# A new issue order for all five engines of a fused Infini-attention and spectral-filter kernel

## The chip, the cores and the metric

The kernel runs on one core of a Trainium2 chip. The core has a matrix engine (TensorE, in the profile PE, with its weight loads as PEld), three engines for elementwise work (VectorE or DVE, ScalarE or ACT, GpSimd or POOL), and SyncE (SP), which here only issues DMAs. Each engine takes its own queue of instructions strictly in order and waits on semaphores for the others. The metric is the device time of one launch in microseconds.

## The reference

Two branches share one input x of 2048 tokens by 640 channels, and a gate per token mixes them. Branch A is attention with a compressive memory: 32 heads of width 20, four segments of 512 tokens, exact softmax attention inside a segment and a running memory (M, z) over the segments before. Branch B is a two-dimensional spectral filter: a real FFT over tokens and channels, a product with complex weights, and the inverse.

```python
phi = lambda t: jnp.where(t > 0, t + 1.0, jnp.exp(t))
for s in range(N):                      # 4 segments
    logits = jnp.einsum('bhqd,bhkd->bhqk', qs, ks) * scale + mask
    p = _softmax(logits, axis=-1)
    a_dot = jnp.einsum('bhqk,bhkd->bhqd', p, vs)
    num = jnp.einsum('bhld,bhde->bhle', phi(qs), M)
    den = jnp.einsum('bhld,bhd->bhl', phi(qs), z)[..., None] + 1e-06
    outs.append(g * num / den + (1.0 - g) * a_dot)      # g = sigmoid(beta)
    M = M + jnp.einsum('bhld,bhle->bhde', phi(ks), vs)
    z = z + jnp.einsum('bhld->bhd', phi(ks))
a = o @ wo
...
b = irfft2(rfft2(x) * (w_r + 1j * w_i))
g = sigmoid((x * gate_w).sum(-1, keepdims=True))
out = g * a + (1 - g) * b
```

Inputs are bfloat16; the sums run in 32 bits.

## The kernel before

All work is first recorded as a list of operations, without an order: a matmul group into one PSUM bank, one copy out of a bank, one elementwise instruction, one DMA. Each operation knows what it reads and writes, and which engines may do it (one or two). Then `Sched.schedule` (from line 117) turns a list of numbers written out by hand, `Kern.ORDER` (from line 639), into a queue for each engine, and `Sched.emit` writes the instructions with their waits. The value v of the list stands for operation v // 2, and v % 2 says which of its engines does it:

```python
        for v in order:
            o = ops[v // 2]
            o.eng = list(o.alts)[v % 2]
            queue[o.eng].append(o)
```

Three more things follow from the order. First, the PSUM bank of each group: banks 0 to 3 are one slot of four banks for attention scores, banks 4 to 7 are single banks for everything else, and a group may only begin when its bank has been read out. Second, DMAs: a DMA is issued once no more than `WINDOW = 1600000` bytes of earlier ones are outstanding, and 56 semaphores are handed round among them. Third, the form of TensorE's tiles: whole 128 by 128, the 20 by 64 tiles of the scores, or columns of 128 by 32; a few groups may take either of two forms and follow their neighbours (line 565 is a matmul split into columns, line 567 an ordinary one).

*Branch A.* `project`, `proj_tile` and `v_tile` make q, k and v of each segment from the transposed x (xT, brought in by transposing DMAs, line 600). q and k go through DRAM: stores to `qk_scr` (`st_qk`), then DMAs `pad2` (line 602) that write the padded operand `qkp`, each of 40 KB in the first segment, eight of them for one set. phi(k) is transposed by a DMA into `pkn` (`pkT`, line 600). `qk_unit` does one of 73 score units into the four-bank slot, ACT turns it into exponentials (`ex`, line 1357), POOL masks the diagonal (line 1391), and `pv_flipped` and `pv_group` multiply by v. With the flipped form the denominators are gathered through DRAM (`dnc`) and inverted in one instruction (line 1294, `den_rec`); products then normalise the output (line 1645). `mem_read` (lines 1224 to 1229) and `mem_update` (operation `mupd`) work on the memory, and an addition joins both parts of the output (lines 1438 and 1655).

*Branch B.* `fft` is a chain of matmuls with constant tables (`fcat`, `big`, `tt`): the folded input (lines 972 and 977), stages F1 and D, the product with the weights (lines 1548 and 1553, `W_mul` and `W_add`), stage T and back; `fft_out` makes even and odd halves and adds them into G (line 1602, `sum_Db`).

*The end.* `finish_tile` multiplies the attention output by wo, the gated G by its last table, into one bank; `final` copies that out to `ot` (line 577 on ACT, line 579 on DVE), and DMAs store it. The gate table of each segment (`gate_tab`, line 1094) is broadcast by a DMA `ld_g`.

Copies out of PSUM may be done by ACT or DVE (`copy_alts`), many additions by DVE or POOL (`either`).

Of the kernel before, what the change touches and what calls it, by code (L numbers as in the profile page):

```python
# [510 lines left out]
class Kern:  # L511
# [84 lines left out]
    def dma(self, dst, src, nbytes, r, w, prio, tr=False, name="", after=(), queue="sp"):  # L596
# [43 lines left out]
        23, 0, 78, 28, 92, 74, 2, 4, 24, 6, 8, 26, 10, 12, 76, 14, 30, 16, 18, 20, 46, 34, 180, 44, 184, 52, 220, 208, 36, 196, 210, 186, 48, 198,  # L640
        212, 42, 188, 190, 222, 38, 94, 200, 202, 96, 204, 192, 224, 206, 99, 226, 195, 228, 214, 101, 216, 231, 542, 32, 262, 219, 103, 544, 302,
        264, 304, 80, 306, 368, 106, 308, 82, 266, 104, 370, 84, 268, 1618, 66, 270, 132, 372, 272, 386, 87, 310, 570, 274, 313, 388, 280, 572, 68,
        282, 276, 134, 50, 390, 284, 88, 286, 54, 108, 392, 394, 58, 90, 374, 110, 288, 396, 828, 830, 136, 558, 290, 833, 113, 376, 560, 822, 824,
        379, 834, 139, 827, 1620, 416, 836, 418, 70, 420, 140, 422, 838, 72, 424, 114, 496, 426, 498, 117, 294, 500, 502, 1622, 504, 550, 506, 246,
        296, 552, 342, 278, 248, 56, 232, 142, 234, 120, 292, 250, 252, 118, 344, 316, 122, 354, 318, 254, 298, 314, 346, 320, 356, 256, 124, 348,
        300, 144, 236, 350, 126, 238, 322, 352, 240, 1842, 128, 358, 168, 242, 360, 1844, 130, 362, 146, 244, 1624, 364, 1626, 1812, 149, 258, 1846,
        380, 1848, 1850, 1628, 546, 400, 40, 1852, 816, 818, 1630, 821, 1632, 260, 1814, 1634, 1816, 156, 366, 846, 848, 1818, 170, 850, 1642, 398,
        840, 150, 842, 1644, 332, 158, 844, 1820, 1646, 336, 152, 1648, 1822, 402, 1650, 154, 810, 404, 1662, 1652, 894, 382, 812, 1664, 172, 340,
        814, 1666, 384, 896, 328, 882, 160, 884, 898, 1668, 1658, 334, 888, 887, 890, 175, 1670, 338, 892, 566, 1673, 330, 442, 562, 1636, 444, 326,
        446, 1880, 1638, 448, 324, 568, 176, 1882, 508, 162, 510, 450, 512, 164, 514, 452, 454, 1656, 167, 516, 456, 458, 1654, 460, 518, 462, 179,  # L650
        470, 520, 412, 1884, 464, 1886, 522, 1888, 466, 472, 410, 474, 584, 1890, 476, 468, 478, 912, 578, 914, 480, 900, 902, 916, 608, 580, 905,
        414, 1868, 1870, 564, 610, 1872, 408, 1874, 1876, 1684, 1660, 934, 870, 1878, 1686, 182, 872, 1640, 1688, 406, 876, 875, 878, 574, 1690,
        1892, 880, 1692, 600, 586, 1695, 1896, 1676, 576, 1898, 602, 482, 1894, 484, 1900, 554, 1902, 938, 1904, 428, 906, 1906, 582, 430, 932, 908,
        486, 488, 548, 911, 490, 432, 434, 492, 436, 1680, 1854, 918, 2310, 494, 438, 920, 1678, 1856, 1858, 525, 440, 1860, 556, 1862, 922, 924,
        926, 588, 858, 860, 658, 928, 60, 863, 594, 1864, 1698, 526, 852, 1866, 804, 596, 1674, 854, 864, 806, 660, 936, 1934, 857, 1922, 1936, 1924,
        930, 1926, 1928, 1938, 1930, 62, 1940, 590, 1932, 2306, 694, 1942, 1724, 593, 1944, 604, 1726, 1946, 628, 1696, 1682, 866, 1022, 1948, 780,
        606, 630, 1728, 869, 1908, 782, 612, 1910, 1730, 1700, 1912, 1914, 1916, 784, 696, 1732, 788, 1918, 940, 942, 1734, 662, 1920, 1951, 614,
        944, 948, 950, 664, 1742, 1736, 952, 792, 947, 1953, 794, 955, 1738, 786, 1702, 1704, 796, 698, 960, 2308, 800, 956, 790, 962, 1706, 1740,
        529, 616, 798, 978, 1954, 1708, 958, 666, 598, 618, 1710, 980, 1957, 986, 531, 982, 988, 1713, 802, 1794, 990, 1796, 1959, 993, 1798, 1714,
        1800, 1718, 1756, 1716, 1016, 532, 985, 624, 620, 1758, 964, 626, 1802, 1720, 1760, 966, 534, 998, 1744, 1020, 1804, 1762, 536, 636, 1764,  # L660
        1000, 994, 1754, 1766, 1072, 638, 1074, 1076, 670, 996, 1824, 808, 1078, 974, 1024, 640, 672, 1774, 1988, 1002, 1776, 540, 1990, 642, 1778,
        977, 1780, 1722, 1004, 1782, 1770, 648, 1992, 632, 1994, 1784, 678, 1960, 651, 1768, 1970, 622, 1750, 1026, 2350, 680, 1972, 1786, 1028,
        1790, 1030, 2352, 1974, 644, 1033, 2354, 538, 968, 1976, 700, 1012, 1110, 970, 1772, 1006, 1015, 1748, 1008, 634, 1788, 686, 973, 646, 1104,
# [1064 lines left out]
```

## Time and profile before

| | us |
|---|---|
| median of 3 runs | 236.89 |
| lowest and highest | 235.61, 237.70 |
| the profiled execution | 235.84 |
| its span in the profile | 233.7 |

The profile shows one execution. Times are microseconds from the start of its span. For each engine it gives busy time; an entry of a timeline reads: start, length, engine, line, operation, result and inputs, count, and in brackets the idle time just before with the operation that ended it. SPq and ACTq are DMAs as their engine issues them; the length is that of the issue, and the landing comes later. A matmul's end is modelled, and successive matmuls overlap by some 0.1 us, so entries of TensorE overlap as well. A group of instructions reads: line, engine, operation, result and inputs with their shapes, count, then busy us in all and mean ns of one, then idle time before it and who ended it.

### The profile page before, as it was taken

The page shows a single profiled execution, that of the slowest core. Times are in us where ns is not written, and L with a number is a line of the kernel's source. Part 1 is how long each engine was busy: PE and PEld are TensorE (multiplying, and loading weights), DVE is VectorE, ACT ScalarE, POOL GpSimd, SP SyncE. Part 2 cuts the span into 40 slices and gives each one's busy share as a digit, 9 for nine tenths or more (in the row PEclk, how much of TensorE's full clock was granted, in tenths as well). Part 3 has the DMA queues.
Part 4 walks back from the last instruction along what each step waited for, and adds up shares of the span by engine and source line. Part 5 has one row for each costly group of instructions (what it writes and reads, how often), then busy time and mean ns, then how long its engine had stood idle before and what let it go on. Part 6 is the DMA issues. An engine that isn't in the chain of part 4 may idle for free.

```text
span 233.7 us, 10364 instructions
## 1 busy us (share of the span) xinstructions
PE 222.5 (95%) x4381; PEld 142.2 (61%) x4395; DVE 191.4 (82%) x486; ACT 194.0 (83%) x215; POOL 148.6 (64%) x301
## 2 busy tenths in 40 slices
PE   7899999999999999999999999899999989999994
PEld 2575676776546666554657554555645457767794
DVE  0299998789999997999999889999799975955364
ACT  2179898889999899999999989999989879788720
POOL 8153138366668985477766878488998758487700
PEclk9999999999999999999999999999999999999999
DMA  6999945999998978456984764685799743222524
GB/s 153 289 330 281 222 150 159 207 195 242 214 201 193 231 186 248 111 148 200 234 176 123 215 196 118 207 181 190 215 155 212 202 126 93 76 78 59 181 95 123
DMA packets 59265, 42.18 MB, mean 180 GB/s; under 512 B 30228, under 2 KB 55380, under 8 KB 59220
## 3 DMA queue, kind: packets, MB, share of 16 engines
q1 hardware_dynamic: 58180, 40.96, 69.7%
q8 instruction: 34, 0.56, 1.0%
q10 hardware_dynamic: 1040, 0.57, 0.9%
q14 instruction: 11, 0.09, 0.1%
HBM read 23.32 MB, written 12.30 MB: 152 GB/s over the span
## 4 chain that ended last, share of the span: by engine, by line
PE 68%; DVE 15%; ACT 5%; SPq 4%; DMA 4%; issue 2%; POOL 1%; DVEq 0%
PE psum L567 61%; PE psum L565 7%; ACT ex L1357 4%; DVE Pt L1548 3%; SPq L602 2%; DMA xsb<-in_A_x_dram 2%; DVE Cp L579 2%; SPq L600 2%; DMA dnc<-u_scr 2%; DVE G L1602 2%; DVE Bt L579 1%; DVE mem L1229 1%; DVE ub L579 1%; DVE Yt L1553 1%; ACT ub L577 1%
## 5 line engine op out<-in xcount | busy, mean ns | idle before, releaser
L1357 ACT ACTIVATE ex<-psum 128x2048 bf16<-128x2048 f32 (+1 forms) x73 | 135.2, 1853 | 11.7 <-PE psum L567 10.6
L1391 POOL TENSOR_SCALAR_AFFINE_SELECT ex<-ex 128x256 bf16<-128x256 bf16 (+3 forms) x224 | 104.5, 485 | 43.2 <-ACT ex L1357 12.1
L567 PE MATMUL psum<-qkp 20*64 20x64 bf16 (+5 forms) x1280 | 31.9, 270 | 1.8 <-DVE qkp L579 0.7
L567 PE MATMUL psum<-xT,wk 128*128 128x256 bf16 (+1 forms) x280 | 33.2, 273 | 0.3 <-DVE mem L1229 0.2
L567 PE MATMUL psum<-xT,wq 128*128 128x512 bf16 (+1 forms) x121 | 27.7, 380 | 1.6 <-DMA xT<-in_A_x_dram 0.8
L567 PE MATMUL psum<-wv,xT 128*32 128x321 bf16 (+3 forms) x385 | 27.8, 301 | 0.0
L1548 DVE TENSOR_TENSOR Pt<-psum,Wt 128x642 bf16<-128x642 f32 x32 | 25.4, 815 | 0.4 <-PE psum L567 0.3
L567 PEld LDWEIGHTS psum<-qkp 20*64 20x64 bf16 x1280 | 13.7, 103 | 17.4 <-ACT ex L1357 11.2
L567 PEld LDWEIGHTS psum<-xT,wk 128*128 128x128 bf16 (+1 forms) x280 | 20.0, 97 | 6.4 <-issue 1.6
L977 POOL TENSOR_TENSOR xsb<-xf 128x320 bf16<-128x320 bf16 (+2 forms) x11 | 8.4, 771 | 20.4 <-DVE xf L972 11.4
L567 PE MATMUL psum<-big,Cp 128*128 128x321 bf16 (+1 forms) x96 | 18.9, 303 | 1.1 <-DVE G L1602 0.9
L565 PE MATMUL psum<-wo,oU 128*32 128x320 bf16 x460 | 19.6, 299 | 0.0
L1187 DVE TENSOR_TENSOR va<-psum,ebx 128x320 bf16<-128x320 f32 x32 | 15.0, 483 | 4.3 <-PE psum L567 1.9
L567 PE MATMUL psum<-big,Ac 128*128 128x161 bf16 (+2 forms) x96 | 17.1, 257 | 0.7 <-DVE Pt L1548 0.3
L567 PE MATMUL psum<-ex,va 128*32 128x64 bf16 (+3 forms) x576 | 17.4, 256 | 0.1
L567 PEld LDWEIGHTS psum<-wv,xT 128*32 128x32 bf16 (+1 forms) x385 | 13.5, 96 | 6.3 <-issue 1.5
L567 PE MATMUL psum<-tt,Yt 128*128 128x256 bf16 (+1 forms) x96 | 16.3, 275 | 0.4 <-POOL Yt L1553 0.3
L567 PEld LDWEIGHTS psum<-ex,va 128*32 128x32 bf16 x576 | 10.9, 96 | 8.8 <-issue 0.7
L972 DVE TENSOR_TENSOR xf<-xsb 128x640 bf16<-128x640 bf16 x16 | 8.2, 515 | 9.1 <-DMA xsb<-in_A_x_dram 9.0
L1144 ACT ACTIVATE et<-qu 128x512 bf16<-128x512 bf16 x25 | 15.4, 625 | 0.2 <-DVE phq L1157 0.2
L1602 DVE TENSOR_TENSOR G<-eo,psum 128x320 bf16<-128x320 f32 x32 | 14.9, 480 | 0.7 <-PE psum L567 0.2
L579 DVE CAST Bt<-psum 128x322 bf16<-128x322 f32 x26 | 13.2, 517 | 2.1 <-PE psum L567 1.8
(102 smaller groups left out, 394.1 us busy)
## 6 DMA issues: line engine op xcount, KB each, us to landing
qkp<-qk_scr SPq DMA_DIRECT2D x28, 160.0 KB
tt<-tab_tt SPq DMA_DIRECT2D x8, 512.0 KB, 4.7
qk_scr<-qu SPq DMA_DIRECT2D x12, 256.0 KB, 3.8
u_scr<-ub SPq DMA_DIRECT2D x12, 256.0 KB, 4.3
xsb<-in_A_x_dram SPq DMA_DIRECT2D x8, 320.0 KB, 5.6
oU<-u_scr SPq DMA_DIRECT2D x15, 128.0 KB, 3.3
out_dram<-ot SPq DMA_DIRECT2D x12, 160.0 KB
Wt<-in_B_w_r_dram SPq DMA_DIRECT2D x16, 80.2 KB, 4.0
```

What stands on the lines that cost most here:

```text
L565: h = e.matmul(dst, wt, r_, start=st, stop=sp_, **{**kw, "tile_position": (0, q), "skip_group_check": True})
L567: h = e.matmul(o_, l_, r_, start=st, stop=sp_, **kw)
L579: alts["dve"] = (lambda e: e.tensor_copy(dst(), src()), 67 + 1.04 * n, 68.0)
L600: return e.dma_start_transpose(d_, s_)
L972: self.either(lambda e, r=r, op=op: e.tensor_tensor(xf.ap(r * 642, [321, 2], [1, 320]), xs.ap(o, [D, 2], [1, 320]), xs.ap(o + 320, [D, 2], ...
L977: self.either(lambda e, dst=dst, src=src, d0=d0, n=n, op=op: e.tensor_tensor(xs.ap(o + dst, [D, 2], [1, n]), xf.ap(src + d0, [321, 2], [1, ...
L1144: self.one("act", lambda e: e.activation(et.ap(0, [1, L]), qsl(), ACT.Exp), L, [qb], [b("et", pi_)], late, fix=95, name="phi_exp")
L1187: self.one("dve", lambda e: e.tensor_tensor(va.ap(i * H * VW + h0 * VW, [VW, nh], [1, DH]), self.ps(bank, 0, [DH, nh], [1, DH]), self.ebx. ...
L1357: self.one("act", lambda e, d=d, q=q: e.activation(self.ex.ap(*d), self.ps(bank, *q), ACT.Exp, scale=SC), 2048 if kind < 2 else 512 * n, [ ...
L1391: self.one("pool", lambda e: e.affine_select(self.ex.ap(*d, p0=p0, np_=np_), self.ex.ap(*q, p0=p0, np_=np_), [[0, 4], [1, n]], ALU.is_ge, ...
L1548: self.one("dve", lambda e, ri=ri, Pt=Pt, Wt=Wt, wo_=wo_, bank=bank: e.tensor_tensor(Pt.ap(ri * 322, [644, 2], [1, KD]), self.ps(bank, 0, ...
L1602: self.one("dve", lambda e, q=q, n2=n2, bank=bank, eo=eo: e.tensor_tensor(self.G.ap(n2 * D + 639 * q, [1 - 2 * q, 320]), eo.ap(q, [1, 320] ...
```

## The change

Only the list `Kern.ORDER` is replaced. The operations, their instructions, the tables, the buffers and all constants of the scheduler are the same. The new list names the same 2311 operations in another sequence, fourteen of them with their other engine. A few lines of the diff, which has 97 on one side and 96 on the other (332 is the `pad2` that the prediction speaks of, 324 the `pkT` near it):

```diff
     ORDER = (
-        23, 0, 78, 28, 92, 74, 2, 4, 24, 6, 8, 26, 10, 12, 76, 14, 30, 16, 18, 20, 46, 34, 180, 44, 184, 52, 220, 208, 36, 196, 210, 186, 48, 198,
...
-        840, 150, 842, 1644, 332, 158, 844, 1820, 1646, 336, 152, 1648, 1822, 402, 1650, 154, 810, 404, 1662, 1652, 894, 382, 812, 1664, 172, 340,
...
-        446, 1880, 1638, 448, 324, 568, 176, 1882, 508, 162, 510, 450, 512, 164, 514, 452, 454, 1656, 167, 516, 456, 458, 1654, 460, 518, 462, 179,
...
-        4524, 4512, 4510, 4554, 4556, 4527, 4566, 4508, 4558, 4568, 4560, 4546, 4570, 4548, 4572, 4563, 4574, 4542, 4544, 4577, 4506, 4580, 4582,
-        4584, 4578,
+        23, 0, 78, 28, 92, 74, 2, 4, 24, 6, 8, 26, 10, 12, 76, 14, 30, 16, 18, 20, 46, 34, 180, 44, 184, 48, 196, 186, 52, 188, 198, 190, 36, 220,
...
+        322, 1630, 244, 1814, 168, 400, 1850, 1632, 821, 260, 149, 1816, 1634, 398, 846, 130, 1852, 258, 848, 1818, 170, 850, 840, 842, 324, 1642,
...
+        510, 330, 512, 514, 164, 454, 1654, 1658, 448, 450, 176, 456, 458, 332, 452, 167, 1880, 516, 414, 460, 462, 518, 1882, 384, 470, 408, 520,
...
+        4532, 4613, 4502, 4598, 4486, 4534, 4505, 4488, 4520, 4616, 4618, 4522, 4491, 4550, 4552, 4614, 4536, 4538, 4512, 4554, 4556, 4506, 4541,
+        4564, 4620, 4524, 4566, 4510, 4558, 4527, 4568, 4508, 4560, 4570, 4572, 4542, 4563, 4544, 4574, 4577, 4546, 4548, 4578, 4584, 4582, 4580,
```

By engine, the lengths of the queues before and after are: PE 1066 and 1066, DVE 486 and 488, ACT 223 and 221, POOL 297 and 297, SP 239 and 239. The operations that go to another engine:

| operation | line | from | to |
|---|---|---|---|
| three `final` | 577, 579 | ACT | DVE |
| two `final` | 579, 577 | DVE | ACT |
| one `ev_D` (copy of a spectral stage, `Bt`) | 577, 579 | ACT | DVE |
| another `ev_D` | 579, 577 | DVE | ACT |
| one `ev_oT3` (copy of a transposed output, `oTl`) | 577, 579 | ACT | DVE |
| two `W_add` | 1553 | DVE | POOL |
| one addition to the attention output, at the end | 1438 | DVE | POOL |
| another such addition | 1438 | POOL | DVE |
| one fold of the input | 977, 972 | POOL | DVE |
| one small operation of the gate | 1060 to 1080 | POOL | DVE |

Operations that keep their place in their queue: 365 of 1066 on PE, 141 of 218 on ACT, 91 of 480 on DVE, 48 of 294 on POOL and 37 of 239 on SP. The mean move is 1.7 places on PE, 1.9 on DVE, 3.0 on POOL and 4.6 on SP. The form of TensorE's tiles changes 202 times in the new order, 206 times in the old one.

183 rows, old and new, of the table ORDER are left out of this document.

## The prediction

> **What bounds the kernel now.** I read the page's totals, its slices and the chain that ended last; then the busy time by windows and TensorE's waits; then the queue of SyncE and TensorE's timeline wherever a moved operation lies. From the page:
>
> ```profile
> span 233.7 us, 10364 instructions
> PE 222.5 (95%) x4381; PEld 142.2 (61%) x4395; DVE 191.4 (82%) x486; ACT 194.0 (83%) x215; POOL 148.6 (64%) x301
> PEclk9999999999999999999999999999999999999999
> q8 instruction: 34, 0.56, 1.0%
> PE 68%; DVE 15%; ACT 5%; SPq 4%; DMA 4%; issue 2%; POOL 1%; DVEq 0%
> ```
>
> The reader is to see an almost full TensorE at its full clock: 233.7 − 222.5 = 11.2 us is all that it idles, and an order can win little else, since the matmuls stay the same. Where that idle time is, TensorE's waits and two windows (columns: window, length, then busy us of PE, PEld, DVE, ACT, POOL; clock, DMA share, GB/s) tell:
>
> ```profile
> PE psum L567 <- DVE G L861: 1.3, 1, 1.3
> PE psum L567 <- DVE G L1602: 0.9, 1, 0.9
> PE psum L567 <- DMA xT<-in_A_x_dram: 0.8, 1, 0.8
> PE psum L567 <- DVE qkp L579: 0.7, 1, 0.7
> PE psum L567 <- ACT ex L1357: 0.6, 2, 0.4
> ...
> 105.00:125.00 20.00, 18.77 (x321) 11.02 (x321) 19.42 (x55) 19.04 (x18) 14.36 (x32) 1.00 0.78 188
> ...
> 220.00:233.70 13.70, 10.46 (x300) 9.21 (x288) 6.82 (x19) 2.73 (x6) 1.64 (x4) 0.98 0.36 108
> ```
>
> 1.3 and 0.8 us are the first wait and the first transposed tile of x, which the change leaves where they are; 13.70 − 10.46 = 3.2 us lie around the last matmuls and stores. So about 11.2 − 1.3 − 0.8 − 3.2 = 5.9 us are there to be won inside. The window 105 to 125 shows why a search finds it hard: DVE 19.42 and ACT 19.04 of 20 us, beside PE at 18.77.
>
> **The change, part by part.** Read out by engine, the new list has the same 1066 TensorE operations and the same 239 on SP. The exponentials' 73 score units keep their sequence; 365 TensorE operations keep their place and the others move by 1.7 places in the mean. SP is dealt anew: 37 of 239 keep their place, the largest moves are 24 places later and 38 earlier. I took SP first, since there an operation that is moved drags others with it.
>
> *The padded q and k of the first segment.* One of the eight DMAs that write the padded operand qkp goes from place 30 of SP to place 39, behind the transposing transfer of pkn that was at place 38, the seven others and a store:
>
> ```profile
> 29.25 4.86 SPq L602 DMA_DIRECT2D qkp<-qk_scr  x8
> 34.15 1.21 SPq L600 DMA_TRANSPOSE pkn<-phk  x1
> 35.46 0.54 SPq L602 DMA_DIRECT2D qk_scr<-qu  x1
> 36.11 2.48 SPq L602 DMA_DIRECT2D qkp<-qk_scr  x4
> ...
> L602 SPq DMA_DIRECT2D qkp<-qk_scr x12: 281/360/1835, 29.2 to 38.2; - x12
> ...
> 36.64 0.42 PE L567 MATMUL psum<-qkp 20*64 20x320 bf16 x16
> ...
> out_dram<-ot SPq DMA_DIRECT2D x8, 40.0 KB, 1.6
> qk_scr<-qu SPq DMA_DIRECT2D x12, 256.0 KB, 3.8
> ```
>
> In the new order there lie ahead of the piece the seven others (4.86 less a median issue of 0.36: 4.5, the one long issue of 1835 ns kept among them), the transfer (1.21), the store (0.54) and 0.1 of gaps: it is issued at 29.25 + 6.35 = 35.6. Landing: 1.6 us for the same 40 KB elsewhere, 3.8 for a larger transfer as the long end. So 35.6 + 1.6 = 37.2 to 35.6 + 3.8 = 39.4, against TensorE's need at 36.64, with the same matmuls ahead. The stall is 0.6 to 2.8 us; I take 0.9, near the end with the 40 KB row, since it has the size and SP issues little else at that time. TensorE takes its queue in order, so all of it counts unless a later wait hides it.
>
> The Trainium skill ("DMA: Bandwidth & Descriptors", Anatomy of one DMA) puts a fixed cost of about 2.0 us on every DMA, most of it the receipt of the write; by it the estimate is 35.6 + 2.0 = 37.6 and a stall of 1.0, where the row says 1.6 and 0.6.
>
> *Other late data.* The memory update below reads pkn, whose transfer moves one place down, behind an issue:
>
> ```profile
> 39.40 1.32 SPq L600 DMA_TRANSPOSE pkn<-phk  x1
> ...
> pkn<-phk SPq DMA_TRANSPOSE x9, 4.7
> ...
> 44.71 0.29 PE L567 MATMUL psum<-fcat,xsb 128*128 128x128 bf16 x2
> 44.83 0.43 PE L567 MATMUL psum<-va,pkn 128*128 128x154 bf16 x4
> ```
>
> By the median of such transfers it lands at 39.40 + 4.7 = 44.1, 0.7 ahead of 44.83. By the queue ahead of it it is issued 1.0 later: 0.3 late, but TensorE is by then 0.9 late itself, so 0 (0.3 if the first stall isn't there). A table for the T stage at 131 us and another memory update at 73 us come 0.3 to 0.4 late by the same walk down the queue. For all of these together I take +0.2, ends 0 and 1.1.
>
> *Tile forms.* The rows that follow hold TensorE (first four) and DVE (last two) around the denominators of a late segment:
>
> ```profile
> 186.29 0.45 PE L567 MATMUL psum<-big,Cp 128*128 128x321 bf16 x2
> 186.67 0.32 PE L565 MATMUL psum<-wo,oU 128*32 128x320 bf16 x4
> ...
> 190.18 0.72 PE L567 MATMUL psum<-big,Cp 128*128 128x321 bf16 x4 [0.94 <-DVE G L1602]
> 190.83 0.43 PE L567 MATMUL psum<-qkp 20*64 20x512 bf16 x12
> ...
> 188.30 0.95 DVE L1294 RECIPROCAL dnr<-dnc 128x128 f32<-128x128 bf16 x1 [1.58 <-DMA dnc<-u_scr]
> 189.17 0.95 DVE L1602 TENSOR_TENSOR G<-eo,psum 128x320 bf16<-128x320 f32 x2
> ```
>
> Four matmuls and a change of form take 190.83 − 190.18 = 0.65, two and a change 186.67 − 186.29 = 0.38; so a pair of matmuls is 0.27, and 0.11 remains for a change of form. The new order has 202 of them instead of 206: −0.44, none of it hidden on a full engine.
>
> *The reciprocal at 188.30.* DVE waits 1.58 us for the gathered denominators, computes 0.95, and only then frees the bank for which TensorE waits 0.94. In the new order a normalising product and the first of the two sums of G go ahead of the reciprocal; DVE does them in the wait and the bank is free sooner. The ends are 0 and −0.94; I take −0.4, because the second sum still follows the reciprocal and is late next.
>
> *The wait at 148.69 and the tail.*
>
> ```profile
> 148.69 0.42 PE L567 MATMUL psum<-qkp 20*64 20x320 bf16 x16 [0.43 <-ACT ex L1357]
> ...
> L1357 ACT ACTIVATE ex<-psum 128x2048 bf16<-128x2048 f32 x71 | 133.2, 1876 | 11.6 <-PE psum L567 10.6
> ```
>
> Some matmuls of the spectral stage move ahead of the score unit at 148.69 and fill its 0.43; they push the unit back, and the exponential behind it, so I count −0.3 (ends −0.43 and 0). In the tail an addition to the attention output goes from DVE to POOL and two transposes come earlier, but the last matmuls follow one another densely: −0.2, ends −0.7 and +0.5, the latter POOL's longer 790 against 317 ns from the rows below. The gate table for the last tiles is loaded six SP places later and still made ahead of its first matmul by my walk down the queues, so nothing (up to +1 if its load, too, lands late).
>
> *The engine changes.* Their prices by shape, one form on its two engines each:
>
> ```profile
> L1553 POOL TENSOR_TENSOR Yt<-Pt 128x321 bf16<-128x321 bf16 x16 | 11.6, 727 | 1.0 <-DVE phq L1156 0.4 <-DVE dn L1224 0.3 <-DVE Pt L1548 0.2
> L1553 DVE TENSOR_TENSOR Yt<-Pt 128x321 bf16<-128x321 bf16 x16 | 5.2, 328 | 0.4 <-PE psum L567 0.3
> L579 DVE CAST ot<-psum 128x320 bf16<-128x320 f32 x16 | 7.4, 489 | 6.5 <-PE psum L565 4.5 <-PE psum L567 1.5 <-DMA out_dram<-ot 0.4
> L577 ACT ACTIVATE ot<-psum 128x320 bf16<-128x320 f32 x16 | 6.5, 435 | 1.7 <-PE psum L567 0.9 <-PE psum L565 0.8
> L1438 DVE TENSOR_TENSOR on<-on,mem 128x320 bf16<-128x320 bf16 x7 | 1.9, 317 | 0.0
> L1438 POOL TENSOR_TENSOR on<-on,mem 128x320 bf16<-128x320 bf16 x1 | 0.8, 790 | 0.0
> ```
>
> Five of the fourteen are copies of output tiles (three to DVE, two to ACT: 54 ns each), two W additions and two attention additions go to POOL (+0.40 and +0.47 us each, if someone waits; DVE gets 0.3 back each), two are a pair of spectral copies that swap engines, and three small ones remain. POOL is busy 64%, and ACT and DVE 82 and 83%: as work this is a fair deal, as latency it is a small loss. Taken as 0, ends −0.6 (four times 0.3 off a full DVE, half of it felt) and +0.8 (both W additions late at the T stage).
>
> **The sum.** +0.9 + 0.2 − 0.44 − 0.4 − 0.3 − 0.2 + 0 = −0.24 us. The profiled execution took 235.84 us, its span 233.7, so 2.1 lie outside; the sum gives a span of 233.5 and 235.6 for this run. The median of the three runs before, 236.89, is 1.05 above the profiled one, and by the median the sum gives 236.65. I predict 236.6: no change. One per cent, 2.4 us, is about what a measurement here tells from none.
>
> **The rivals.** *Slower: the instruction blocks hit the wrong issues.* The long pad issue of 1835 ns coincides with a packet of the instruction queue q8; so does a transposing transfer that took a microsecond more than the one behind it:
>
> ```profile
> 66.40 2.28 SPq L600 DMA_TRANSPOSE pkn<-phk  x1
> ...
> 69.82 1.25 SPq L600 DMA_TRANSPOSE pkn<-phk  x1
> ```
>
> An SP issue is stretched by 1.0 to 1.5 us where a block is fetched. There are 34 such packets; in the order before the slack ahead of qkp and pkn takes them up, in the new one they fall on other issues. Each that falls ahead of an operand with less slack costs 0.9 to 1.3 of a full TensorE, as in the first part. One is in the sum; from the third the gains of 1.3 us are eaten, and with four the time is 236.65 + 3 × 1.1 = 239.9. For it: the two rows above, and 202 issues with new places. Against it: where I walked down the new queue, only one operand came late by more than 0.5.
>
> The Trainium skill ("Runtime: NRT & Kernel Launch", Instruction fetch mechanics) holds the opposite: the fetch of the next block is mostly hidden behind the rate at which instructions are issued; by that rule this rival has no price and the time stays at the forecast. The 1835-ns issue speaks against it, though that it coincides with a packet is no proof of the cause.
>
> *Faster: the idle time inside goes.* If a block falls elsewhere and no issue at 31 is stretched, the late piece of qkp leaves 1.5 us earlier, at 34.1, lands at 35.7 and stalls nothing. The first two terms (+1.1) fall away, and half of the 5.9 us of idle time inside, 2.9 instead of the 0.9 in my sum, can go: 236.65 − 1.1 − 2.0 = 233.5. For it: the new order puts free work into both of the waits that I looked at. Against it: DVE and ACT at 95 to 97% between 105 and 125, where a place that one operation gains is another's loss.
>
> *The change does nothing.* All stays in the same waits; 236.9, which is inside the forecast.
>
> **How the numbers follow.** Forecast, no change, 0.44 (own range 235.1 to 238.6: below, the qkp stall at 0.6 instead of 0.9, no other late data, the wait for G wholly gone and the tail at its good end, −0.3 − 0.2 − 0.5 − 0.5; above, the stall at 2.8, +1.9); faster 0.30, centred on 233.5, of which about 0.25 lies below 234.5; slower 0.26, centred on 239.9, of which 0.22 lies above 239.3. The forecast's own flanks give 0.02 and 0.03. Faster by over 1%: 0.27; within: 0.48; slower: 0.25. With about a tenth left out on either side the range is 233.4 to 239.9.
>
> **What would show it.** The score unit that now starts at 36.64 would show a wait of 0.6 us or more for the DMA of qkp; without it the first term is wrong. TensorE's wait for G (0.9) should be half, and that at 148.69 gone. SP's long issues should lie elsewhere than at 31 and 66. TensorE's busy time should stay within 0.5 us of 222.5; idle time under 8 us would mean the faster case, over 13 the slower one. The prediction falls if one new wait of over 2 us stands in TensorE's list, or if none of the old ones is left.

## The result, and the profile after

| | old order | new order |
|---|---|---|
| median, us (21 runs each, in turns on the same chips) | 235.88 | 237.23 |
| lowest and highest, us | 234.62, 237.70 | 236.38, 241.15 |
| the profiled execution, us | 235.84 | 237.99 |
| its span, us | 233.7 | 236.0 |

The new order is slower: ratio 1.0073, 95% interval 1.005 to 1.0096, or 1.7 us (1.2 to 2.3). That is inside 1% and inside the range, but the forecast had −0.24 us and the sign is the other. The old median of 236.89 in the prediction came from three runs; 21 give 235.88. The new profiled execution lies 0.8 us above its own median and the old one on its median, so that the traces show 2.3 us where the runs show 1.7. The ratios leave out runs over 1.5% above the fastest of their kernel; of the 20 of the new order that are left, four have a mean granted clock of 0.993 and take 238.9 to 239.4 us, and without these four their mean is 0.4 us lower.

The page of the new order, the same lines as before:

```profile
span 236.0 us, 10369 instructions
PE 224.7 (95%) x4395; PEld 142.0 (60%) x4395; DVE 192.7 (82%) x488; ACT 193.1 (82%) x213; POOL 149.3 (63%) x301
PEclk9999999999999999999999999999999999999999
q8 instruction: 34, 0.56, 1.0%
PE 80%; DVE 9%; DMA 3%; ACT 2%; SPq 2%; issue 2%; POOL 0%
```

TensorE's idle time is 236.0 − 224.7 = 11.3 us, by the pages as before (11.2). The two can't be compared so closely, however: the old trace has records of 4381 matmuls and the new one of 4395, and the 14 that are missing, all of the q projection, don't count as busy. So the rise of the busy time from 222.5 to 224.7, which the prediction had excluded, doesn't prove more work, and the old idle time may be too high. The waits are others in any case (us in all, times, longest):

```profile
PE psum L567 <- DMA qkp<-qk_scr: 1.7, 1, 1.7
PE psum L567 <- DVE G L860: 1.3, 1, 1.3
PE psum L567 <- DMA xT<-in_A_x_dram: 0.9, 1, 0.9
PE psum L567 <- issue: 0.9, 3, 0.3
PE psum L567 <- DVE qkp L579: 0.7, 1, 0.7
PE psum L567 <- ACT ex L1356: 0.4, 2, 0.2
```

The 0.94 for G is gone, and the 0.43 for an exponential. A single new one of 1.7 stands at the head, for the DMA of qkp. Where the time comes in shows best when one takes the start of the same score unit in each trace, since the sequence of the 73 units is the same (starts in us, worked out from the traces; the last column is the new order with the first 40 places of SP's queue as in the old one, of which more below):

```
unit                  old     new   new − old    with 40 old places   − old
 5                   32.31   32.64    +0.33            32.16          −0.15
 6                   36.64   38.77    +2.13            36.73          +0.09
12                   56.09   58.31    +2.22            56.69          +0.60
38                  125.36  127.43    +2.07           125.83          +0.47
46                  146.11  148.51    +2.40           146.94          +0.83
47                  148.69  151.08    +2.39           149.52          +0.83
56                  171.67  174.86    +3.19           172.51          +0.84
62                  187.16  190.38    +3.22           188.10          +0.94
63                  190.83  192.94    +2.11           190.66          −0.17
66                  198.84  201.11    +2.27           198.44          −0.40
67                  201.40  204.04    +2.64           201.06          −0.34
73                  217.60  220.11    +2.51           217.79          +0.19
end of the span     233.7   236.0     +2.3            233.8           +0.1
```

At the sixth unit 1.8 us come in at once. The difference dips to 1.4 at unit 9, and from unit 11 to unit 38 it stays between 1.9 and 2.4: score unit, exponential and score unit follow one another at a fixed pace, and a delay that has got into this chain stays in it. Behind it the new order loses 1.1 more up to unit 56, wins 1.1 at unit 63 and ends where it was.

### The profile page after: what moved, and what is told of

The parts are those of the page before. It is cut to its first block, busy times and chain, and to the rows that moved or that the text cites. A ratio compares the mean times of both kernels' runs of the same rounds, so it can differ in the third digit from the quotient of the medians.

```text
span 236.0 us, 10369 instructions
## 1 busy us (share of the span) xinstructions
PE 224.7 (95%) x4395; PEld 142.0 (60%) x4395; DVE 192.7 (82%) x488; ACT 193.1 (82%) x213; POOL 149.3 (63%) x301
## 4 chain that ended last, share of the span: by engine, by line
PE 80%; DVE 9%; DMA 3%; ACT 2%; SPq 2%; issue 2%; POOL 0%
PE psum L567 72%; PE psum L565 8%; DMA xsb<-in_A_x_dram 2%; SPq L600 2%; ACT ex L1356 2%; DVE Pt L1547 1%; DVE G L1601 1%; DVE Bt L579 1%; DMA qkp<-qk_scr 1%; DVE ub L579 1%; DVE mem L1231 1%; DVE Macc L1466 0%; DVE xf L971 0%; DVE dn L1226 0%; DVE va L1186 0%
## 5 line engine op out<-in xcount | busy, mean ns | idle before, releaser
L567 PE MATMUL psum<-qkp 20*64 20x64 bf16 (+5 forms) x1280 | 32.4, 270 | 3.7 <-DMA qkp<-qk_scr 1.7
L567 PE MATMUL psum<-xT,wq 128*128 128x512 bf16 (+1 forms) x135 | 31.3, 380 | 0.9 <-DMA xT<-in_A_x_dram 0.9
L567 PE MATMUL psum<-wv,xT 128*32 128x321 bf16 (+3 forms) x385 | 27.0, 301 | 0.1
L976 POOL TENSOR_TENSOR xsb<-xf 128x320 bf16<-128x320 bf16 (+2 forms) x10 | 7.6, 764 | 22.3 <-DVE xf L971 13.2
L565 PE MATMUL psum<-wo,oU 128*32 128x320 bf16 x460 | 20.1, 300 | 0.0
L567 PE MATMUL psum<-big,Cp 128*128 128x321 bf16 (+1 forms) x96 | 18.3, 302 | 0.1
L567 PE MATMUL psum<-big,Ac 128*128 128x161 bf16 (+2 forms) x96 | 16.5, 258 | 0.6 <-ACT Bt L577 0.3
L567 PEld LDWEIGHTS psum<-xT,wq 128*128 128x128 bf16 (+1 forms) x135 | 9.7, 97 | 8.8 <-issue 1.5
```

The lines of the kernel that those rows point to most:

```text
L565: h = e.matmul(dst, wt, r_, start=st, stop=sp_, **{**kw, "tile_position": (0, q), "skip_group_check": True})
L567: h = e.matmul(o_, l_, r_, start=st, stop=sp_, **kw)
L976: self.either(lambda e, dst=dst, src=src, d0=d0, n=n, op=op: e.tensor_tensor(xs.ap(o + dst, [D, 2], [1, n]), xf.ap(src + d0, [321, 2], [1, ...
```

## The experiments

The kernels are either order with a part of one engine's queue taken from the other. Numbers are those of the operations (value // 2). SP's places 13 to 39, of which most of the experiments are made, old above new:

```diff
 places 13 to 23
-xT 809, ld_x 25, ld_x 27, ld_x 29, xT 810, xT 811, ld_x 28, st_qk 146, st_qk 158, st_qk 157, pkT 150
+xT 809, xT 810, ld_x 25, st_qk 146, ld_x 27, ld_x 29, st_qk 158, xT 811, ld_x 28, pkT 150, st_qk 157
 places 24 to 39
-st_qk 122, st_qk 129, ld_gw 20, st_qk 130, st_qk 183, st_qk 199, pad2 166, pad2 168, pad2 170, pad2 164, pad2 167, pad2 169, pad2 165, pad2 163, pkT 162, st_qk 827
+ld_gw 20, st_qk 122, st_qk 130, st_qk 199, st_qk 129, pkT 162, st_qk 183, pad2 164, pad2 170, pad2 168, pad2 167, pad2 169, pad2 163, pad2 165, st_qk 827, pad2 166
```

Ratios are to the old order on the same chip, with their 95% intervals; 0.1% is 0.24 us.

### Is the loss in SP's queue, and where?

**new_sp40old**: the new order, SP's places 0 to 39 old.

```diff
 SP:
-new[0:40] + new[40:]
+old[0:40] + new[40:]
```

> The new order on all engines, with the first 40 places of SP's queue as in the old order (the same 40 DMAs in the old sequence). Theory A: the loss is made there, the last padded piece of qkp lands at 38.7 instead of in time, and the chain of scores and exponentials carries the 2.1 us to the end; then this kernel is 1.7 to 2.2 us faster than the new one, about 0.2 to 0.7 us under the old one, and the wait of 1.73 us for qkp is under 0.3. Theory B: the late piece is absorbed by waits that would come anyway, and the loss lies in many small waits behind it; then it is at most 0.7 us faster than the new one, still 0.5 us or more above the old one.

Ratio 0.9976 (0.9955 to 0.9997); span 233.8 against 236.0. TensorE's list of waits, and its sixth unit in the timeline:

```profile
PE psum L567 <- DVE G L861: 1.3, 1, 1.3
PE psum L567 <- DMA xT<-in_A_x_dram: 0.7, 1, 0.7
PE psum L567 <- issue: 0.6, 3, 0.3
PE psum L567 <- DMA tt<-tab_tt: 0.5, 1, 0.5
```

```profile
36.73 0.42 PE L567 MATMUL psum<-qkp 20*64 20x320 bf16 x16 [0.17 <-issue]
```

The wait for qkp is gone, and with it the loss. Theory A.

**old_sp40new**: the reverse, the old order with SP's places 0 to 39 new.

```diff
 SP:
-old[0:40] + old[40:]
+new[0:40] + old[40:]
```

> The old order on all engines, with the first 40 places of SP's queue as in the new order. Theory A: slower than the old one by 1.7 to 2.2 us, with a wait for the DMA of qkp of 1.3 to 1.8 us at the sixth score unit. Theory B: slower by 0.7 us at most.

Ratio 1.0117 (1.0055 to 1.0179): as theory A has it, if anything more. Its interval is wide. Its profile (span 239.4) shows a wait of 2.9 us for qkp, where 1.3 to 1.8 were expected, and TensorE's granted clock is 0.50 from 39.3 to 46.1, of which more in the last section.

**new_spold** and **old_sp206new**: the same with SP's whole queue, or nearly.

```diff
 SP of new_spold:
-new
+old
 SP of old_sp206new:
-old[0:206] + old[206:]
+new[0:206] + old[206:]
```

> The new order on PE, DVE, ACT and POOL, with the whole of SP's queue as in the old order. Theory A: within 0.4 us of the kernel with only the first 40 places restored. A third theory, C, that the later places of SP cost as well (late operands at 73 and 131 us and others): 0.5 us or more faster than that kernel. Theory B: within 0.7 us of the new one.

> The old order on PE, DVE, ACT and POOL, with the first 206 of 239 places of SP's queue as in the new order (the last 33 as in the old, since all 239 cannot be combined with the old order at the end). Theory A: as the kernel with 40 new places, within 0.4 us. Theory C: 0.5 us or more slower than that kernel. Theory B: within 0.7 us of the old one.

Ratios 1.0138 (1.01 to 1.0177) and 1.037 (1.0311 to 1.0429). Both are far worse than with 40 places. The second goes the way of theory C, but the first goes against all three: with the old sequence in its later places the new order gets slower, not faster. In the second TensorE waits 2.9 us at once for a product of POOL; in the first no single wait stands out. So the later places of SP aren't what costs the new order its time; each sequence of them belongs to its own order.

### Which of the 40 places?

**new_sp24old**, **new_sp24_40old** and, in the old order, **old_sp24new**, **old_sp24_40new**: one half of the 40 places exchanged.

```diff
 SP of new_sp24old:       old[0:24] + new[24:]
 SP of new_sp24_40old:    new[0:24] + old[24:40] + new[40:]
 SP of old_sp24new:       new[0:24] + old[24:]
 SP of old_sp24_40new:    old[0:24] + new[24:40] + old[40:]
```

> The new order with the first 24 places of SP's queue (loads of x, the second transposed tile, first stores) in the old sequence; places 24 to 39 stay new. Theory A1: the wait for qkp stays at 0.9 or more, gain under 0.9 us. Theory A2: SP is 1.3 us earlier at place 24, the wait falls to 0.5 or less, gain 1.2 us or more.

> The new order with places 24 to 39 of SP's queue (the stores of q and k, the transfer and the eight padded pieces) in the old sequence; the first 24 stay new. Theory A1: wait for qkp under 0.4 us, 1.3 to 2.0 us faster than the new one. Theory A2: wait of 0.9 or more, gain under 0.9.

> The old order with the first 24 places of SP's queue as in the new order. If the loads and early stores are the larger half: 1.0 to 1.7 us slower than the old one (ratio 1.004 to 1.007), with the lateness of SP at place 24 being 1 us or more. If the padded pieces' half is the larger one: under 0.7 us slower.

> The old order with places 24 to 39 of SP's queue as in the new order. If the loads and early stores are the larger half: a wait for qkp of under 0.6 us and under 0.9 us slower than the old one. If the padded pieces' half is the larger one: a wait of 0.6 us or more and 1.0 to 1.7 us slower.

With the repeated measurement of new_sp24old and new_sp40old (below) the times make a square in each order:

| places 0 to 23 | places 24 to 39 | rest old | rest new |
|---|---|---|---|
| old | old | 1 | 0.9976, 1.0009 |
| old | new | 1.0023 (0.9985 to 1.0061) | 0.9990 (0.9957 to 1.0023), 1.0055 (1.0017 to 1.0093) |
| new | old | 1.0068 (1.0032 to 1.0104) | 1.0050 (1.0021 to 1.0079) |
| new | new | 1.0117 (1.0055 to 1.0179) | 1.0073 (1.005 to 1.0096) |

The first 24 places cost 0.7 to 0.9% in the old order and some 0.5 to 0.6% in the new one, taking the mean of the repeats; places 24 to 39, where the transfer of pkn stands ahead of the padded pieces, cost 0.2 to 0.5%. All eight differences have the same sign, though a single one has an interval of 0.3 to 0.7% either way. That the first 24 places cost time is clear of this in all four cases; what places 24 to 39 cost is clear in none of them alone. The two measurements of one kernel, 0.9990 and 1.0055, lie further apart than their intervals allow, so the shares of the halves are rough. The larger half is the one to which the prediction gave no term. In the trace of new_sp24_40old the wait at the sixth unit is gone, and a wait of 0.60 us for the next set of qkp comes at 44.88.

What the first half does is seen in old_sp24new, in which TensorE waits for a transposed tile of x whose transfer the new order puts later among the loads, and is 1.4 us late at the fifth unit already:

```profile
27.94 0.31 PE L567 MATMUL psum<-wv,xT 128*128 128x320 bf16 x1 [0.73 <-DMA xT<-in_A_x_dram]
```

In the new order itself PE has other work there, and it is SP that carries the delay: at place 24 it is at 27.16 instead of 25.88, 1.3 us late.

**new_sp24old_b**: new_sp24old once more.

> The same kernel as new_sp24old (first 24 places of SP restored, places 24 to 39 new), for an execution near its own median. If SP's head is what the larger half costs: SP issues the last padded piece 0.8 us or more earlier than the new order does (36.70), and TensorE's wait for qkp is 0.9 us or less. If the disturbed look was typical: an issue of 1.5 us or more that overlaps an instruction block lies right at that piece again, and the wait is over 1.5 us. Ratio to the old one 0.997 to 1.002.

Ratio 1.0055 (1.0017 to 1.0093). Both profiled executions of this kernel took longer than the median of their measurement (238.55 against 236.62, and 239.71 against 238.05 us), so they show what can happen with this sequence, not what happens in most runs. In the second one SP is earlier, as it was meant to be: it reaches place 24 at 25.82, and the last padded piece of the first set, at place 39, is issued at 34.63, 2.1 us ahead of the new order. Yet TensorE waits 2.25 us for it (the chain, then TensorE):

```profile
34.63 3.94 DMA qkp<-qk_scr
38.58 0.04 issue
38.62 2.44 PE psum L567 x39
```

```profile
38.62 0.42 PE L567 MATMUL psum<-qkp 20*64 20x320 bf16 x16 [2.25 <-DMA qkp<-qk_scr]
```

It is the landing that is late, 3.94 us behind the start of the issue instead of 2.03. By the semaphore's updates the piece lands in ten parts, nine of them at 36.57 to 36.75 and the tenth at 38.58. A packet of the instruction queue q8 is on its way from 35.34 to 36.81, and the tenth part comes 1.8 us after its end. In the first trace it is the same, although SP is no earlier there than in the new order (27.16 at place 24): issue at 36.17, nine parts landed by 38.53, packet from 36.64 to 38.34, the tenth part 1.7 us after its end at 40.07, a wait of 2.9. An issue of SP that meets the packet is held as well, but it belongs to the next set (the two issues of the first row are 0.27 and 1.69 us long; the second begins at 35.53 and ends at 37.22):

```profile
35.21 2.00 SPq L602 DMA_DIRECT2D qkp<-qk_scr  x2
37.26 0.46 SPq L602 DMA_DIRECT2D qk_scr<-qu  x1
```

That the packet delays the tenth part is inferred from these two traces. Of the 24 runs of both measurements 8 lie above 238.5 us, against 1 of the 24 of new_sp40old; whether they are the ones in which the packet falls like this isn't shown.

### One transfer, three loads

**new_pkT**: only the transfer pkT 162 behind the last piece. **new_loads**: only the three loads back between the transposing transfers. **new_loads_pkT**: both. **old_loads** and **old_loads_pkT**: the same two moves the other way in the old order.

```diff
 SP of new_pkT:
-st_qk 129, pkT 162, st_qk 183, pad2 164, ..., st_qk 827, pad2 166
+st_qk 129, st_qk 183, pad2 164, ..., st_qk 827, pad2 166, pkT 162
 SP of new_loads:
-xT 809, xT 810, ld_x 25, st_qk 146, ld_x 27, ld_x 29, st_qk 158
+xT 809, ld_x 25, ld_x 27, ld_x 29, xT 810, st_qk 146, st_qk 158
 SP of old_loads:
-xT 809, ld_x 25, ld_x 27, ld_x 29, xT 810, xT 811
+xT 809, xT 810, ld_x 25, ld_x 27, ld_x 29, xT 811
 SP of old_loads_pkT, besides:
-st_qk 183, st_qk 199, pad2 166, ..., pad2 163, pkT 162
+pkT 162, st_qk 183, st_qk 199, pad2 166, ..., pad2 163
```

> The new order with one DMA of SP moved: the transposing transfer of pkn that stands 10 places ahead of the last padded piece of qkp goes right behind it. Its own issue took 1.58 us. Theory A1 (the place of this transfer is most of the cause): the wait for qkp falls from 1.73 to under 0.4 us and the kernel is 1.3 to 1.8 us faster than the new one. Theory A2 (SP is late there because of what happens in its first 24 places, 1.3 us by then): the wait stays at 1.0 or more and the gain is under 0.7 us, since an issue stretched by an instruction block takes the freed time.

Ratio 1.0065 (1.0033 to 1.0097), no better than the new order. In the profile the wait is cut as A1 says, but a quarter of the way on something else turns up (TensorE, TensorE, ACT, and the chain that led there):

```profile
37.47 0.42 PE L567 MATMUL psum<-qkp 20*64 20x320 bf16 x16 [0.20 <-DMA qkp<-qk_scr]
61.10 0.39 PE L567 MATMUL psum<-xT,wq 128*128 128x512 bf16 x1 [0.98 <-ACT qu L577]
```

```profile
60.45 0.60 ACT L577 ACTIVATE qu<-psum 128x512 bf16<-128x512 f32 x1 [1.69 <-DMA qk_scr<-qu]
```

```profile
56.05 4.37 DMA qk_scr<-qu
```

A store of q that took 4.4 us to land holds the buffer that ACT wants to write, and TensorE stands 0.98 for it: of the 1.5 us won by unit 12, 0.14 are left at unit 15. With all 40 places restored TensorE waits 0.3 for ACT at most. Neither theory had this.

> The new order with the three loads of x that follow the second transposing transfer of the second segment put between the first and the second one, as in the old order; nothing else moves. Theory A2 (two transposing transfers back to back hold SP for 5.6 us where the loads between them cost nothing, and all that follows on SP is 1.2 us late): SP reaches the padded pieces about 1.2 us earlier, the wait for qkp falls from 1.73 to 0.6 us or less, and the kernel is 1.0 to 2.0 us faster than the new one (ratio to the old one 0.999 to 1.003). Theory A3 (the lateness comes from the issues that an instruction block stretches, wherever they are): the wait stays at 1.2 or more, ratio 1.005 or more.

> As the one before, and the transposing transfer of pkn goes behind the last padded piece as well. If these two places are the whole cause: no wait for qkp over 0.2 us and the same time as with the first 40 places restored (ratio 0.996 to 0.999). If other places among the 40 count: 0.5 us or more above that.

> The old order with the second transposing transfer of the second segment moved ahead of three loads of x, as in the new order. Theory A2: SP is 1.2 us late at the padded pieces, which uses up the 1.2 us that the last piece had in hand: a wait for qkp of 0 to 0.5 us, 0 to 0.6 us slower than the old one (ratio 1.000 to 1.003). Theory A3: as the old one.

> As the one before, and the transposing transfer of pkn ahead of the eight padded pieces. Together they make the last piece 2.5 to 3 us later than in the old order, with 1.2 in hand: a wait for qkp of 1.3 to 1.8 us, and 1.3 to 2.2 us slower than the old one (ratio 1.0055 to 1.009). If the new order's loss were elsewhere: under 0.7 us.

Ratios 1.0027 (0.9989 to 1.0065), 1.0001 (0.9967 to 1.0034), 1.0068 (1.0034 to 1.0102) and 1.0044 (1.0002 to 1.0086). The mechanism of theory A2 falls. That the transfers stand back to back holds nothing up: the second one ends at 19.2 in the new order and at 19.5 in the old one, loads between them or not. And in new_loads SP begins the padded pieces at 33.57 instead of 33.48, since two issues, of 2.92 and 1.93 us, met packets of q8 (the second is the store that met one in the new order, too); the wait for qkp is 1.99. But the time goes down by 0.46%, into the range that A2 gave and some 60% of the loss, though the interval of this difference is 0.44% either way. In the old order three later loads alone cost as much as the first 24 places, without a wait for qkp at the sixth unit: in the trace of old_loads this unit is 0.6 us behind the old order, unit 12 is 1.2 behind and unit 56 is 1.8 behind. So the loads of x matter by another way than the one I had named, and which it is stays open. The two moves together bring back the time of the old order (1.0001), and in this trace no wait for qkp is in the list: within the interval of 0.3% one transfer and three loads hold the whole loss. In the old order both of them cost 1.0 us, less than the 1.3 to 2.2 that were expected and not more than the loads alone; the wait for qkp is 0.76.

### The reciprocal, and a table

**old_denrec**: the old order, on DVE both sums of G ahead of the reciprocal. **new_sp40old_noden**: new_sp40old, the sum of G and the product behind the reciprocal again. **new_sp56old**: 16 more places of SP old.

```diff
 DVE of old_denrec:
-den_rec 1479, sum_Db 1957, sum_Db 1958, normal 2025
+sum_Db 1957, sum_Db 1958, den_rec 1479, normal 2025
 DVE of new_sp40old_noden:
-normal 2025, ev_Db 1953, normal 2033, sum_Db 1957, den_rec 1479, sum_Db 1958
+ev_Db 1953, normal 2033, den_rec 1479, sum_Db 1957, sum_Db 1958, normal 2025
 SP of new_sp56old:
-old[0:40] + new[40:]
+old[0:56] + new[56:]
```

> The old order with two operations of DVE moved: both sums of G that stand behind the reciprocal of the late denominators go ahead of it. If TensorE is the bound there, its wait of 0.94 us at 189.2 goes and the kernel is 0.7 to 1.0 us faster than the old one (ratio 0.996 to 0.997). If the chain behind it (score unit, exponential, normalising products) is the bound, the wait turns up again behind and it is faster by 0.3 us at most.

Ratio 0.9990 (0.9958 to 1.0022). The profiled execution is one of 239.39 us, against a median of 235.92. TensorE in it:

```profile
189.28 0.71 PE L567 MATMUL psum<-big,Cp 128*128 128x321 bf16 x4
...
191.17 0.46 PE L565 MATMUL psum<-wo,oU 128*32 128x320 bf16 x8 [0.33 <-DVE oU L1655]
...
195.84 0.46 PE L567 MATMUL psum<-G,fbg 128*32 128x320 bf16 x4 [1.96 <-ACT ot L577]
```

The wait of 0.94 is gone, and the score unit behind it starts at 189.92 instead of 190.83; 0.33 comes back a little later, where the output waits for its addition. (For the 1.96, ACT waits for a store of the output that lands late.) Between 0.7 and 1.0 us were expected of the one case and at most 0.3 of the other; the interval holds both.

> The kernel with the first 40 places restored, and on DVE the first sum of G and the normalising product put behind the reciprocal again, as in the old order. If the reordering there is what the new order gains: TensorE waits 0.5 to 1.0 us for G again at 188 to 190, and the kernel is 0.5 to 1.0 us slower than with 40 places alone (ratio 0.999 to 1.002). If not: no such wait, the same time.

Ratio 1.0019 (0.9987 to 1.0051). No wait for G came back, though DVE has the old sequence (DVE's timeline, then TensorE's):

```profile
187.83 0.95 DVE L1294 RECIPROCAL dnr<-dnc 128x128 f32<-128x128 bf16 x1
188.69 0.95 DVE L1602 TENSOR_TENSOR G<-eo,psum 128x320 bf16<-128x320 f32 x2
```

```profile
189.94 1.13 PE L567 MATMUL psum<-big,Cp 128*128 128x321 bf16 x7
```

The reciprocal doesn't wait here. Why, SP tells; the gather of the denominators in the old and the new order:

```profile
184.60 0.51 SPq L602 DMA_DIRECT2D dnc<-u_scr  x1
```

```profile
186.71 0.51 SPq L602 DMA_DIRECT2D dnc<-u_scr  x1
```

The gather has the same place on SP in both orders (207), with ten loads of u ahead of it. But between the last store of u and the gather stand four of these loads in the old order and three in the new one, and against the score unit that follows (187.16 and 190.38) it is issued 2.56 us ahead in the old order and 3.67 in the new one; in new_sp40old_noden it is 3.34. In these traces the earlier gather takes the wait away, and in old_denrec DVE's sequence does it by itself.

> The new order with the first 56 places of SP's queue as in the old one (16 more than before; the table of the T stage goes one place earlier). If the wait of 0.46 us for this table at 53 us is on the path: 0.2 to 0.5 us faster than with 40 places (ratio 0.995 to 0.997). If the chain behind hides it: the same, 0.9976 within 0.15%.

Ratio 1.0032 (1.0001 to 1.0063), span 234.0. The ratio is above what either case gave. The wait for the table goes from the list and unit 11 starts 0.71 us earlier than in new_sp40old, but of this 0.25 are left at unit 12 and none at the end. The table isn't a term.

**new_sp40old_b**: new_sp40old once more, on another chip.

> The same kernel as new_sp40old: ratio to the old one 0.996 to 0.999 if the new order outside SP's first 40 places is a small gain, 0.999 to 1.002 if the first measurement was luck.

Ratio 1.0009 (0.998 to 1.0038). Its profile shows how little is fixed in this region: the same program, but a load of u ahead of the gather takes 1.83 us to issue, the gather comes only 2.80 ahead of the score unit, DVE waits 0.91 for it, and TensorE 0.54 for G:

```profile
191.10 1.01 PE L567 MATMUL psum<-big,Cp 128*128 128x321 bf16 x6 [0.54 <-DVE G L1602]
```

With both measurements the version with 40 places restored is as fast as the old order; that it is faster isn't shown.

## Why the prediction was wrong

The sum had 0.24 us less, and the runs have 1.7 more. The stall for qkp came out 0.8 larger than it was taken, and of the gains of 1.34 us most didn't come.

**The padded q and k: the step that failed.** Its place, its mechanism and its sign were right. The chain of the new order, followed back from its end, goes through it:

```profile
36.70 2.03 DMA qkp<-qk_scr
38.73 0.04 issue
38.77 1.43 PE psum L567 x37
```

The term was +0.9 and the wait is 1.73, inside the ends of 0.6 to 2.8. The landing of 2.03 is longer than the 1.6 of the 40 KB row that I leaned on, which is that of a store of the output; in the old trace the eight pieces themselves land 1.7 to 3.8 us behind the start of their issues, by their semaphores' updates. The estimate from the Trainium skill ("DMA: Bandwidth & Descriptors", Anatomy of one DMA), about 2.0 us, agrees with this landing (the page gives it for DMAs that GpSimd issues, which the prediction left out; this one is issued by SP). The larger part is the issue, 36.70 instead of 35.6; against both, TensorE itself comes to the unit 0.4 later. "It is issued at 29.25 + 6.35 = 35.6" lets the pieces begin where they begin in the old order. They don't; SP in the new order, first at the two transfers, then at the pieces:

```profile
13.57 5.65 SPq L600 DMA_TRANSPOSE xT<-in_A_x_dram  x2
19.27 0.58 SPq L602 DMA_DIRECT2D xsb<-in_A_x_dram  x1
19.89 0.43 SPq L602 DMA_DIRECT2D qk_scr<-q  x1
20.37 2.10 SPq L602 DMA_DIRECT2D xsb<-in_A_x_dram  x2
...
30.08 1.58 SPq L600 DMA_TRANSPOSE pkn<-phk  x1
31.70 1.68 SPq L602 DMA_DIRECT2D qk_scr<-q  x1
33.48 2.74 SPq L602 DMA_DIRECT2D qkp<-qk_scr  x7
36.27 0.39 SPq L602 DMA_DIRECT2D qk_scr<-qu  x1
36.70 1.33 SPq L602 DMA_DIRECT2D qkp<-qk_scr  x3
```

SP is hardly ever idle from 13.6 to 38, so each earlier place counts as much as those beside the pieces, and the first 24 places had been dealt anew as well. In the old order three loads of x are issued by 17.8, and here they are at 19.3 to 22.5:

```profile
16.28 1.53 SPq L602 DMA_DIRECT2D xsb<-in_A_x_dram  x3
17.86 2.93 SPq L600 DMA_TRANSPOSE xT<-in_A_x_dram  x2
```

By the square of experiments these first places make some 60 to 80% of the loss, roughly. My sum had nothing for them. SP's lateness at place 24, 1.3 us, accounts for the later issue of the last piece; the moves of the loads show that it doesn't explain all that these places cost.

**Other late data, +0.2.** The list has no wait of 0.2 us or more for the memory updates or the table.

**Tile forms, −0.44.** Four changes fewer were made, but no step of the table of units shows them apart; they weren't tried alone, and the 0.11 us for a change of form stays an estimate.

**The reciprocal, −0.4.** In the two traces it is −1.1 (unit 62 to 63). The mechanism was half right: the wait goes, but through an earlier gather as much as through DVE's sequence, and in an execution of the new order with SP's first 40 places restored half of it is there again.

**The wait at 148.69, −0.3.** The end that I gave as possible came: 0. The wait is gone and the matmuls fill it, yet the unit stands 2.40 us behind the old order before and 2.39 after it. What the unit waited for was the exponential, and that came no earlier.

**The tail, −0.2.** From unit 73 to the end of the span the new order gains 0.2.

**The engine changes, 0.** TensorE's waits in the new trace name none of the fourteen operations. The prediction miscounted there: one addition to the attention output goes to POOL and another one comes back to DVE; both W additions do go to POOL.

**What was in no term.** Between units 38 and 56 the new order loses another 1.1 us (0.4 with the 40 places restored). It isn't in the waits: TensorE is idle for 1.5 us in this stretch in the new order and for 1.7 in the old one, and the rest is busy time, with 845 matmuls on record against 840; why it is longer stays open. Another 0.8 comes between units 65 and 67, where TensorE stands twice for no reason that the profile shows ("issue", 0.31 and 0.22). Together the sum of the gains, 1.34 us by the forecast, came to between −0.2 and 0.6: that is what the two measurements with 40 places restored leave.

**The rivals.** The slower one named the right queue, and issues that lengthen where an instruction block comes are in the traces (below), but it asked for four of them and 239.9 us. Two lie ahead of the pieces here (1.63 at 20.37 and 1.68 at 31.70), and in the old order one lies among the pieces (1.83 at 31.51); how much of the 1.1 us by which the last piece is issued too late comes from them wasn't set apart. The rule that stood against it in the Trainium skill ("Runtime: NRT & Kernel Launch", Instruction fetch mechanics), that such fetches are mostly hidden, speaks of the engine that fetches; for SP's issues it doesn't hold in these traces (below). The faster one fell: neither the span nor the idle time of the trace is smaller.

## What to carry to other kernels

Where one in-order queue is busy without a break up to a wait, cost a reordering by walking that queue from its last idle moment, not from the moved operation: every place ahead counts, and an error in the start of the walk is an error in the result. In this kernel a stall ahead of a chain that runs at a fixed pace is kept to the end, while of two gaps inside this chain the one of 0.43 won nothing when it was filled and the one of 0.94 did. And a queue that was ordered together with others can't be taken out of one order and put into another: the parts must be exchanged in pieces small enough to keep their neighbours' data in time.

## What the runs showed of the hardware

An issue of SP can be held by a 16 KB packet of the instruction queue that arrives meanwhile, and then ends a fixed time after it. Over all 20 traces of this study there are 235 plain DMA issues under way at the end of a q8 packet (begun at least 0.4 us ahead of it), and 196 of them end 0.35 to 0.45 us after it; the median is 0.38. Not every issue is held: 430 others end while a packet is still under way, 150 of which also began under it. But of the 197 plain issues over 1.0 us long, 183 meet a packet, though packets are under way in only 16% of the time. Some of the held ones, from the old order, the new one and new_sp24old_b:

```
kernel            packet of q8      issue of SP        ends after the packet
old               31.41 to 32.96    31.51 to 33.34     0.38
old               45.12 to 46.08    45.25 to 46.45     0.37
new               20.58 to 21.59    20.37 to 22.00     0.41
new               31.67 to 32.99    31.70 to 33.38     0.39
new               39.16 to 40.44    39.13 to 40.83     0.39
new_sp24old_b     35.34 to 36.81    35.53 to 37.22     0.41
```

So an issue of 0.3 to 0.5 us can become one of 1.2 to 2.0. There are 34 such packets in a trace with some 8790 matmuls and weight loads, and if they bring TensorE's instructions, as this number suggests, which issue is held depends on the order of two engines. That the packet is the cause is inferred from this agreement; no run moved the packets alone.

Behind a long wait TensorE's granted clock can halve. The trace of old_sp40new, whose wait of 2.94 us for qkp ends at 39.70, has 69 matmuls in 6.7 us at a clock of 0.50 and then 274 in 14.0 us at 1.00 (columns as in the windows of the prediction):

```profile
39.30:46.00 6.70, 6.30 (x69) 3.54 (x70) 2.57 (x5) 3.05 (x4) 2.37 (x6) 0.50 0.90 183
46.00:60.00 14.00, 13.99 (x274) 10.07 (x273) 11.27 (x29) 11.85 (x18) 6.41 (x17) 1.00 0.69 136
```

In four of the 20 traces the clock falls to 0.50 in the middle of the work, for 3.4 us (new_sp24old_b, old_denrec), 6.8 (old_sp40new) and 10.2 (old_sp206new), each time 1.8 to 2.9 us after the beginning of a wait of 2.0 to 2.9 us. Two waits of the same length, 2.0 in new_loads and 2.9 in new_sp24old, left it at 1.00, and so did the 1.73 of the new order: the length alone doesn't decide, and the cause is inferred. Where the clock does fall, a late operand costs more than its wait.
